# Transposing K and a mixed activation by DMA instead of by TensorE in a fused sparse-attention and MLP-mixer kernel

## The chip, the cores and the metric

The kernel runs on one core of one Trainium2 chip. The metric is device time in microseconds of one execution. A profiled execution also has a span, from its first to its last instruction, which is a little shorter than its time. The engines are TensorE (PE, with its weight loads PEld), VectorE (DVE), ScalarE (ACT), GpSimd (POOL) and SyncE (SP). Each takes its instructions strictly in program order. SP issues all loads of q, k and v and all stores here; POOL issues the weight loads, because these cast from float32 to float16 on the way; 16 DMA engines carry out both.

## What is computed

Four batches, eight heads, 768 positions, head size 64. Attention is causal and sparse by blocks of 64 keys: each query keeps its own block and the three blocks whose mean key has the largest product with it. The result is fed to a token-mixing and a channel-mixing MLP.

```python
k_rep = k.reshape(B, H, n_blocks, block, D).mean(axis=3)
gate_scores = np.einsum('bhsd,bhnd->bhsn', q, k_rep)
gate_scores = np.where(causal, gate_scores, -1000000000.0)
top_idx = np.argsort(gate_scores, axis=-1)[..., -top_k:]
# mask: own block and the top_k blocks, and position i >= position j
scores = scale * np.matmul(q, k.transpose(0, 1, 3, 2))
scores = np.where(mask, scores, -1000000000.0)
attn = softmax(scores);  x = (attn @ v), heads side by side      # (B, 768, 512)
h = np.maximum(x.transpose(0, 2, 1) @ w_tok1, 0.0) @ w_tok2      # 768 -> 256 -> 768
u = x + h.transpose(0, 2, 1)
h2 = np.maximum(u @ w_ch1, 0.0) @ w_ch2                          # 512 -> 1536 -> 512
return u + h2
```

Inputs and output are float32; the matrix products of the kernel run in float16, except the gate and the transposes of q and k, which are float32.

## The kernel before

**Tiles and stages.** Heads are worked in 16 pairs, i = 0 to 15, four to a batch. For each pair:

- SP loads k and q of the pair (`load_qk`, line 244), each as two DMAs of 192 KB, one for each head, with 256 bytes to a row and head, and v as one DMA of 384 KB (`load_v`, line 253).
- TensorE turns k and q around, six 128x128 float32 transposes each (line 269); ScalarE copies the result out of PSUM into `kt` or `qt` (line 278, two buffers of each); GpSimd casts each head's half into the float16 tiles K and Q that the score matmuls read (line 284).
- VectorE sums `kt` over blocks of 64 keys (`ksum`, line 292) and puts the sums into `ks` (`kcopy`, line 300). The gate is five groups of small float32 matmuls (line 310). VectorE adds the causal bias (line 318), takes the eight largest (line 327), compares with the third (line 334) and makes a float16 bias (line 342), which TensorE transposes (`mask`, line 353) and VectorE copies into the free rows of Q (`put_mask`, line 361). The matching rows of K hold indicators of the blocks, so that the score matmul adds the bias itself.
- Scores come in three groups for each head (line 375), each followed by an exponential on ScalarE (line 388), a triangle mask on VectorE (`diag`, line 395; for pair 0 on TensorE, line 379), the product with v (line 406), and the normalization on VectorE (lines 414, 425).

When a batch's four pairs are done, token mixing follows (`tok1` line 437 and `umix` line 449; for batch 0 in column pieces, lines 468 and 482), then u = x + mix on VectorE (`uadd`, line 457; batch 0 line 491). TensorE transposes u in four steps of six 128x128 float16 transposes (`utr`, line 499), VectorE copies them out (`uput`, line 507). Channel mixing reads uT: 24 groups of `ch1` for a batch (line 518), with their relu on ScalarE or VectorE (lines 528, 530), and 18 groups of `ch2` (line 539), an addition on VectorE (line 547) and the store (line 551). The mixing of one batch is meant to lie beside the attention of the next: it fills TensorE where attention waits for its exponentials. For batch 3 there is no attention left to lie beside.

**What sets the order.** The program order is not the order of the code. `plan` (line 64) is a list scheduler that runs while the program is being built. Every piece of work is an `Op` with an engine, a planned occupation, its dependencies, a priority and the buffers that it takes; `plan` goes through planned time, and on each engine it starts the ready piece of the best priority. The order that comes out is the program order of each engine. The chip then does not choose again: an instruction whose input is late holds everything behind it on its engine. DMAs are planned as one queue, in the order of their planned starts, each with a planned size in time; the names SP and SPO both end up on SyncE. [...]

**Start and end.** `dummy` (line 558) fills TensorE at the start with matmuls of no use (up to `WARM` = 120, until planned time `WARM_END`), which the plan takes at 109 ns each; 79 of them are in the program, 34 ahead of the first transpose. GpSimd sets parts of K and Q to zero first (lines 761 to 768). The weights of the token mixer (lines 570, 571) and of the channel mixer (lines 573, 575) are loaded from GpSimd, at points in its order behind casts of pair 3 and later pairs; two lines (662, 663) keep, in the plan only, the loads of pair 4 behind the second weight load.

Of the kernel before, what the change touches and what calls it, by code (L numbers as in the profile page):

```python
# [9 lines left out]
FP = mybir.dt.float32  # L10
F16 = mybir.dt.float16
# [19 lines left out]
TRI = 1  # L31
EARLY = 1
LEAD = 960.0
WARM, WARM_END = 120, 17000.0
IDLE = 1e9
# [123 lines left out]
def kernel(  # L159
# [24 lines left out]
    sp = ctx.enter_context(tc.tile_pool(name="sb", bufs=1))  # L184
    pp = ctx.enter_context(tc.tile_pool(name="ps", bufs=1, space=bass.MemoryType.PSUM))

    pairs = [(b, h) for b in range(B) for h in range(0, H, 2)]
# [19 lines left out]
    QA = [[sp.tile([128, S], F16, tag=f"Q{r}{x}", name=f"Q{r}{x}") for x in range(2)] for r in range(R)]  # L207
    KAX = [sp.tile([128, R, S], F16, tag=f"K{x}", name=f"K{x}") for x in range(2)]
    KA = [[KAX[x][:, r, :] for x in range(2)] for r in range(R)]
    ks2 = [sp.tile([128, 2 * NB], FP, tag=f"ks{r}", name=f"ks{r}") for r in range(R)]  # L210
# [50 lines left out]


    def transposes(t32, i):
        def f():
            p = ps("big", None, f"t{t32}")
            T["tr", t32, i] = p
            t = T[t32, i]
            for j in range(NJ):
                nc.tensor.transpose(out=p[:, 128 * j:128 * j + 128], in_=t[:, j, :], identity=ident32)  # L269
        return f  # L270

    def evac_t(t32, i):
        def f():
            name = "qt" if t32 == "ql" else "kt"
            t = sb(name, [128, S], FP, f"{name}_{i}")
# [287 lines left out]
    for n in range(WARM):  # L563
        wb.users.append(pe(109, [], IDLE, dummy(n), [wb] if n == 0 else []))
    wq = []
# [12 lines left out]
    for i in range(NP):  # L578
# [7 lines left out]

        for t32, src, off in (("kl", k, 0), ("ql", q, 0.1)):
            bf = Buf(t32)
# [70 lines left out]
    for n, (at, f) in enumerate(wq):  # L659
        after = O["cast", "kt", 3, 1] if n < 2 else O["cast", "qt", 3 + (n - 2) // 2, 1]  # L660
        W.append(op("POOL", 700, 0, [after], at, f, size=2900))
    for t32 in ("kl", "ql"):
        O[t32, FIRST].deps.append(W[1])

    for b in range(B):
# [76 lines left out]
    with tc.manual_schedule():  # L742
# [16 lines left out]
        for x in range(2):  # L759
            lo = 64 * (1 - x)  # L760
            nc.gpsimd.memset(KAX[x][lo:lo + 64, :, :].bitcast(FP), 0.0)
        nc.vector.memset(QA[0][0][64:128, :], 0.0)
# [6 lines left out]
        for r in range(R + 1):  # L769
            nc.vector.memset(V16[r][:, :, :, 64:65], 1.0)  # L770
        tri = const("tri", (MASKV * (1.0 - m0_np)).astype(np.float16), F16, nc.scalar)
        m0 = const("m0", np.stack([m0_np, m0_np], axis=1), F16, nc.scalar)
        ind_dram = nc.inline_tensor(np.ascontiguousarray(np.broadcast_to(ind_np[:, None, :], (NB, R, S))), name="indc").ap()
        for x in range(2):
            lo = 64 * (1 - x)
            nc.scalar.dma_start(out=KAX[x][lo:lo + NB, :, :], in_=ind_dram)

# [35 lines left out]
```

## Time and profile before

| | |
|---|---|
| three runs | 281.8, 286.43 and 286.5 us; median 286.43 |
| the profiled execution | 283.26 us, of which its span is 281.4 us |
| granted TensorE clock, mean | 1.00 |
| TensorE busy | 269.9 us, 96% of the span, 2399 matmuls |
| VectorE, ScalarE, GpSimd busy | 168.6, 142.7 and 78.8 us |
| DMA, SP's queue | 78608 packets, 25.17 MB, 40.7% of 16 engines' span |
| DMA, GpSimd's queue | 3232 packets, 3.93 MB, 8.4% |

The profile page gives busy time by engine, the span in 40 slices with the busy share of each in tenths, the DMA queues, the chain of work that ended last, and the costliest groups of instructions. A group's line has the source line, engine, operation, tiles and shapes, the count, then busy time and mean duration of one, then the idle time of that engine just before these instructions and what ended it. Matmuls overlap one another, so that the mean duration of one is longer than the time by which each moves TensorE on; the pieces of the chain of waits give the latter.

### The profile page before, as it was taken

The numbers are of one execution on the slowest core, as the hardware profiler recorded it, in microseconds if no ns is written. First come the engines' busy times: TensorE is split into PE (matmuls) and PEld (weight loads), VectorE is DVE, ScalarE is ACT, GpSimd is POOL, SyncE is SP. The second block draws the span as 40 slices with busy tenths as digits, with TensorE's granted clock in tenths as the row PEclk, the third lists the DMA queues.
The fourth block names the chain that finished last, engine by engine and source line by source line (L and its number), as shares of the span: only waits on it lengthen the run. The fifth ranks groups of instructions, "written<-read, shape, count | busy, mean of one in ns | idle before, by whom it ended". The sixth has DMA issues, their size and how long they took to land.

```text
span 281.4 us, 6095 instructions
## 1 busy us (share of the span) xinstructions
PE 269.9 (96%) x2399; PEld 180.7 (64%) x2399; DVE 168.6 (60%) x573; ACT 142.7 (51%) x188; POOL 78.8 (28%) x102
## 2 busy tenths in 40 slices
PE   8999799889999999999999999999999999999994
PEld 6987488756778777777786545655455545455543
DVE  4478858897679777979999533336323164233222
ACT  2367977288888998888676703440014410044100
POOL 7577702965443375445422000000000000000000
PEclk9999999999999999999999999999999999999999
DMA  8999999999959499570001111000240001120032
GB/s 174 214 214 224 187 222 211 181 225 194 224 112 170 92 213 201 115 168 2 3 0 40 40 75 75 2 0 0 78 148 0 0 2 75 76 77 0 0 125 101
DMA packets 82780, 29.96 MB, mean 106 GB/s; under 512 B 76200, under 2 KB 79272, under 8 KB 82752
## 3 DMA queue, kind: packets, MB, share of 16 engines
q1 hardware_dynamic: 78608, 25.17, 40.7%
q0 software_dynamic: 3232, 3.93, 8.4%
q10 hardware_dynamic: 912, 0.47, 0.8%
q8 instruction: 19, 0.31, 0.5%
q14 instruction: 9, 0.07, 0.1%
HBM read 27.21 MB, written 6.29 MB: 119 GB/s over the span
## 4 chain that ended last, share of the span: by engine, by line
PE 76%; DVE 14%; POOL 2%; DMA 2%; issue 2%; ACT 2%; DVEq 0%; ACTq 0%; POOLq 0%
PE c L539 21%; PE c L518 21%; PE sps L375 7%; PE aps L406 5%; PE warm L558 4%; PE gps L310 3%; DVE e L395 3%; PE tok L437 3%; PE tkl L269 3%; DMA w<-in_moe_w_tok_dram 2%; PE tql L269 2%; PE ups L449 2%; DVE Q L361 2%; DVE kst L292 2%; PE utps L499 2%
## 5 line engine op out<-in xcount | busy, mean ns | idle before, releaser
L388 ACT ACTIVATE e<-sps 128x1024 f16<-128x1024 f32 (+1 forms) x96 | 84.0, 917 | 16.4 <-PE sps L375 11.1
L518 PE MATMUL c<-uT,wc 128*128 128x256 f16 (+1 forms) x384 | 67.9, 326 | 0.2 <-ACT h L528 0.2
L528 ACT ACTIVATE h<-c 128x512 f16<-128x512 f32 x48 | 28.7, 597 | 74.5 <-PE c L518 64.4
L539 PE MATMUL c<-wc,h 128*128 128x512 f16 (+2 forms) x300 | 65.8, 370 | 0.0
L518 PEld LDWEIGHTS <-wc 128*128 128x128 f16 x384 | 37.3, 98 | 24.2 <-issue 0.4
L375 PE MATMUL sps<-Q,K 128*128 128x512 f16 (+3 forms) x256 | 49.9, 305 | 2.2 <-ACT e L388 1.5
L539 PEld LDWEIGHTS <-h 128*128 128x128 f16 x300 | 28.4, 98 | 29.5 <-issue 0.6
L284 POOL CAST K<-kt 64x768 f16<-64x768 f32 x32 | 26.8, 839 | 58.7 <-ACT kt L278 52.4
L530 DVE TENSOR_SCALAR h<-c 128x256 f16<-128x256 f32 x48 | 20.2, 420 | 35.1 <-PE c L518 35.1
L395 DVE TENSOR_TENSOR e<-e,m 128x256 f16<-128x256 f16 x90 | 31.1, 353 | 14.1 <-ACT e L388 13.5
L547 DVE TENSOR_TENSOR ob<-u,c 128x512 f32<-128x512 f16 (+2 forms) x25 | 16.6, 665 | 33.7 <-PE c L539 33.7
L375 PEld LDWEIGHTS <-K 128*128 128x128 f16 x256 | 22.3, 100 | 16.6 <-ACT e L388 2.0
L284 POOL CAST Q<-qt 64x768 f16<-64x768 f32 x32 | 27.0, 843 | 8.8 <-ACT qt L278 7.4
L406 PE MATMUL aps<-V,e 128*128 128x65 f16 x672 | 27.6, 193 | 0.9 <-DVE e L395 0.7
L406 PEld LDWEIGHTS <-e 128*128 128x128 f16 x672 | 25.6, 98 | 3.5 <-DVE e L395 1.5
L278 ACT COPY kt<-tkl 128x768 f32<-128x768 f32 x16 | 12.8, 799 | 17.4 <-PE tkl L269 7.0
L310 PEld LDWEIGHTS gps<-ks,qt 128*128 128x128 f32 x160 | 19.1, 192 | 2.7 <-DVE ks L300 1.3
L310 PE MATMUL gps<-ks,qt 128*128 128x24 f32 x160 | 20.1, 268 | 0.5 <-ACT qt L278 0.3
L425 DVE TENSOR_TENSOR x<-aps,rc 128x384 f16<-128x384 f32 x32 | 17.7, 553 | 0.6
L361 DVE COPY Q<-bps 12x640 f16<-12x640 f16 x32 | 15.5, 484 | 1.3 <-PE bps L353 0.4
L278 ACT COPY qt<-tql 128x768 f32<-128x768 f32 x16 | 12.8, 800 | 5.0 <-PE tql L269 4.3
L292 DVE TENSOR_REDUCE kst<-kt 128x12 f32<-128x768 f32 x15 | 14.1, 943 | 0.8 <-ACT kt L278 0.8
(52 smaller groups left out, 238.3 us busy)
## 6 DMA issues: line engine op xcount, KB each, us to landing
kl<-in_k_dram SPq DMA_DIRECT2D x32, 192.0 KB, 4.5
ql<-in_q_dram SPq DMA_DIRECT2D x32, 192.0 KB, 4.3
v<-in_v_dram SPq DMA_DIRECT2D x16, 384.0 KB, 5.3
out_dram<-ob SPq DMA_DIRECT2D x23, 256.0 KB, 2.0
wc<-in_moe_w_ch_dram POOLq DMA_DIRECT2D x8, 384.0 KB, 6.9
w<-in_moe_w_tok_dram POOLq DMA_DIRECT2D x2, 384.0 KB, 7.0
out_dram<-ob SPq DMA_DIRECT2D x1, 160.0 KB, 1.8
K<-indc ACTq DMA_DIRECT2D x2, 72.0 KB
```

Of the source, the lines that this page charges most:

```text
L278: nc.scalar.copy(out=t, in_=p[:, 0:S])
L284: nc.gpsimd.tensor_copy(out=dst[i % R][x][lo:lo + 64, :], in_=T[name, i][lo:lo + 64, :])
L310: nc.tensor.matmul(out=g[:, j, :], lhsT=T["qt", i][:, 128 * j + 128:128 * j + 256], rhs=ks2[i % R], start=True, stop=True)
L361: nc.vector.tensor_copy(out=QA[i % R][x][lo:lo + NB, 128:S], in_=T["bps", i][lo:lo + NB, :])
L375: nc.tensor.matmul(out=p[:, off + a:off + a + n], lhsT=KA[i % R][x][:, 128 * kk:128 * kk + 128], rhs=QA[i % R][x][:, q0 + a:q0 + a + n], s ...
L388: nc.scalar.activation(out=e[:, 0:width], in_=T["sps", i, x, g][:, 0:width], func=AF.Exp, scale=scale)
L395: nc.vector.tensor_tensor(out=d, in0=d, in1=m0, op=ALU.mult)
L406: nc.tensor.matmul(out=p[:, jq, :], lhsT=T["e", i, x, g][:, o:o + 128], rhs=V16[i % (R + 1)][:, x, kk, :], start=(kk == 0), stop=(kk == jq))
L518: nc.tensor.matmul(out=p, lhsT=wc1_16[:, cc, 128 * fc:128 * fc + 128], rhs=T["uT", b][:, cc, a:e], start=(cc == 0), stop=(cc == NCC - 1))
L528: nc.scalar.activation(out=T["h2", b][:, fc, a:e], in_=T["c1", b, fc, n], func=AF.Relu)
L530: nc.vector.tensor_scalar(out=T["h2", b][:, fc, a:e], in0=T["c1", b, fc, n], scalar1=0.0, scalar2=None, op0=ALU.max)
L539: nc.tensor.matmul(out=T["c2", b, j, lo], lhsT=T["h2", b][:, fc, 128 * j:128 * j + 128], rhs=wc2_16[:, fc, lo:hi], start=(fc == 0), stop=( ...
```

## The change

For pairs 6 to 15 (`VIA` = 6), k no longer goes through TensorE's transposes. It is loaded with eight consecutive rows to a partition (96 partitions, 2 KB to a row and head). VectorE sums the eight rows (`ksum8`), and one small float32 matmul with a constant 0/1 matrix `blk` finishes the sums over blocks (`ksum_pe`). GpSimd casts k into a padded tile K16 of 256 columns to a position: head 0, its indicator columns and zeros, then zeros and indicator columns, then head 1 (`cast_k8`). SP stores that tile to a scratch in DRAM (`store_k`, 384 KB), and one DMA with transpose (`turn_k`) brings it back as both K tiles of the pair, indicator rows included. The next load of k into a `kt` buffer, the cast and the sums thus share the two `kt` buffers with the kt copies of pairs 0 to 5, which still go the old way.

For batches 1 to 3 (`UVIA` = 1), u is stored to a scratch in DRAM (`store_u`, 768 KB) and brought back transposed by one DMA (`turn_u`); their `utr` and `uput` are gone. `ch1` of these batches waits for that DMA.

All new DMAs are issued by SP, among its loads and stores. In the plan the first 20 fillers now occupy 213 ns instead of 109, so that 61 are in the program instead of 79, 18 of them ahead of the first transpose instead of 34. The two lines that kept the loads of pair 4 behind a weight load in the plan are gone. K becomes one tile instead of two, and its zeroing eight instructions instead of two; two K16 tiles are zeroed and given their indicators at the start of GpSimd's program, and GpSimd loses two casts of 64x768 a pair.

```diff
+VIA = 6
+UVIA = 1
-WARM, WARM_END = 120, 17000.0
+WARM, COLD, WARM_END = 120, 20, 17000.0
...
-    KAX = [sp.tile([128, R, S], F16, tag=f"K{x}", name=f"K{x}") for x in range(2)]
-    KA = [[KAX[x][:, r, :] for x in range(2)] for r in range(R)]
+    KAX = sp.tile([128, R, 2, S], F16, tag="KA", name="KA")
+    KA = [[KAX[:, r, x, :] for x in range(2)] for r in range(R)]
+    K16 = [sp.tile([96, 8, 256], F16, tag=f"K16{y}", name=f"K16{y}") for y in range(2)]
...
+    def load_k8(i):
...
+            t = sb("kt", [128, 2, 8, D], FP, f"k8_{i}")[0:96]
+            T["k8", i] = t
+            nc.sync.dma_start(out=t.rearrange("p g t d -> p g (t d)"),
+                              in_=k[b, h:h + 2].rearrange("g (p t) d -> p g (t d)", t=8))
...
+    def ksum8(i):
...
+            t = sp.tile([96, 2, D], FP, tag="kp", bufs=2, name=f"kp_{i}")
+            nc.vector.tensor_reduce(out=t, in_=T["k8", i].rearrange("p g t d -> p g d t"), axis=AX.X, op=ALU.add)
...
+    def ksum_pe(i):
...
+            p = ps("bank", [128, NB], "kps")
+            nc.tensor.matmul(out=p, lhsT=T["kp", i].rearrange("p g d -> p (g d)"), rhs=blk, start=True, stop=True)
...
+    def cast_k8(i):
...
+            nc.gpsimd.tensor_copy(out=K16[y].rearrange("p t (g c) -> p g t c", g=4)[:, 0:4:3, :, :], in_=T["k8", i])
...
+    def store_k(i):
...
+            t = dram.tile([S, 256], F16, tag=f"ks{i % 2}", name=f"kscr_{i}")
+            nc.sync.dma_start(out=t.rearrange("(p t) c -> p (t c)", t=8), in_=K16[i % 2].rearrange("p t c -> p (t c)"))
...
+    def turn_k(i):
+        return lambda: nc.sync.dma_start_transpose(out=KAX[:, i % R, :, :], in_=T["kscr", i])
...
+    def store_u(b):
...
+            t = dram.tile([S, DM], F16, tag=f"us{b % 2}", name=f"uscr_{b}")
+            nc.sync.dma_start(out=t.rearrange("(j p) c -> p j c", p=128), in_=T["u", b])
...
+    def turn_u(b):
+        def f():
+            T["uT", b] = sb("uT", [128, NCC, S], F16, f"uT_{b}")
+            nc.sync.dma_start_transpose(out=T["uT", b], in_=T["uscr", b])
...
-        wb.users.append(pe(109, [], IDLE, dummy(n), [wb] if n == 0 else []))
+        wb.users.append(pe(213 if n < COLD else 109, [], IDLE, dummy(n), [wb] if n == 0 else []))
...
-        for t32, src, off in (("kl", k, 0), ("ql", q, 0.1)):
+        if i >= VIA:
+            kb = Buf("kt")
+            ld = op("SP", 500, 0, [], pre - 12, load_k8(i), [kb], size=1400)
+            O["ksum", i] = dve(1100, [ld], pre + 1, ksum8(i))
+            nb = Buf("bank")
+            O["kpe", i] = pe(115, [O["ksum", i]], pre + 1, ksum_pe(i), [nb])
+            O["kcopy", i] = dve(260, [O["kpe", i], O.get(("gate", old))], pre + 1, kcopy(i))
...
+            O["castk", i] = op("POOL", 1150, 1200, [ld, O["ki", y], O.get(("kst", i - 2))], pre + 3, cast_k8(i))
+            kb.users += [O["ksum", i], O["castk", i]]
+            O["kst", i] = op("SPO", 600, 0, [O["castk", i], O.get(("cast", "kt", i, 0))], pre + 3.1, store_k(i), size=1600)
+            O["kturn", i] = op("SPO", 600, 0, [O["kst", i]] + last_scores(0) + last_scores(1), pre + 3.2, turn_k(i), size=2500)
+            O["cast", "kt", i, 0] = O["cast", "kt", i, 1] = O["kturn", i]
+        for t32, src, off in (("kl", k, 0), ("ql", q, 0.1))[i >= VIA:]:
...
-    for t32 in ("kl", "ql"):
-        O[t32, FIRST].deps.append(W[1])
...
-        for cc in range(NCC):
+        if b >= UVIA:
+            O["ust", b] = op("SPO", 600, 0, uadds[0], early, store_u(b), size=3000)
+            O["uturn", b] = op("SPO", 600, 0, [O["ust", b]], early, turn_u(b), [tb], size=3500)
+            ub.users.append(O["ust", b])
+        for cc in range(NCC if b < UVIA else 0):
...
-                O["ch1", b, fc, n] = pe((864, 436)[n], [O["uput", b, cc] for cc in range(NCC)] + W[2:6],
+                O["ch1", b, fc, n] = pe((864, 436)[n], ([O["uturn", b]] if b >= UVIA else [O["uput", b, cc] for cc in range(NCC)]) + W[2:6],
```

More of the change, by code (lines that the diff above doesn't have):

```diff
@@ L185 @@
     pp = ctx.enter_context(tc.tile_pool(name="ps", bufs=1, space=bass.MemoryType.PSUM))
+    dram = ctx.enter_context(tc.tile_pool(name="dr", bufs=1, space=bass.MemoryType.DRAM))
     pairs = [(b, h) for b in range(B) for h in range(0, H, 2)]
@@ L260, in cast_v, with f, k16_zero, k16_ind @@
         return f
+    def load_k8(i):
+        b, h = pairs[i]
+        def f():
[3 more added lines that the diff above has]
+                              in_=k[b, h:h + 2].rearrange("g (p t) d -> p g (t d)", t=8))
+        return f
+    def ksum8(i):
+        def f():
+            t = sp.tile([96, 2, D], FP, tag="kp", bufs=2, name=f"kp_{i}")
+            T["kp", i] = t
+            nc.vector.tensor_reduce(out=t, in_=T["k8", i].rearrange("p g t d -> p g d t"), axis=AX.X, op=ALU.add)
+        return f
+    def ksum_pe(i):
+        def f():
+            p = ps("bank", [128, NB], "kps")
+            T["kst", i] = p
+            nc.tensor.matmul(out=p, lhsT=T["kp", i].rearrange("p g d -> p (g d)"), rhs=blk, start=True, stop=True)
+        return f
+    def cast_k8(i):
+        def f():
+            y = i % 2
+            nc.gpsimd.tensor_copy(out=K16[y].rearrange("p t (g c) -> p g t c", g=4)[:, 0:4:3, :, :], in_=T["k8", i])
+        return f
+    def store_k(i):
+        def f():
+            t = dram.tile([S, 256], F16, tag=f"ks{i % 2}", name=f"kscr_{i}")
+            T["kscr", i] = t
+            nc.sync.dma_start(out=t.rearrange("(p t) c -> p (t c)", t=8), in_=K16[i % 2].rearrange("p t c -> p (t c)"))
+        return f
+    def turn_k(i):
+        return lambda: nc.sync.dma_start_transpose(out=KAX[:, i % R, :, :], in_=T["kscr", i])
+    def k16_zero(y):
+        return lambda: nc.gpsimd.memset(K16[y].bitcast(FP), 0.0)
+    def k16_ind(y):
+        def f():
+            for c in (64, 128):
+                nc.gpsimd.tensor_copy(out=K16[y][:, :, c:c + NB],
+                                      in_=blk.rearrange("p (o n) -> p o n", o=1).broadcast_to([96, 8, NB]))
+        return f
+    def store_u(b):
+        def f():
+            t = dram.tile([S, DM], F16, tag=f"us{b % 2}", name=f"uscr_{b}")
+            T["uscr", b] = t
+            nc.sync.dma_start(out=t.rearrange("(j p) c -> p j c", p=128), in_=T["u", b])
+        return f
+    def turn_u(b):
+        def f():
+            T["uT", b] = sb("uT", [128, NCC, S], F16, f"uT_{b}")
+            nc.sync.dma_start_transpose(out=T["uT", b], in_=T["uscr", b])
+        return f
     def transposes(t32, i):
@@ L274, in f @@
             name = "qt" if t32 == "ql" else "kt"
-            t = sb(name, [128, S], FP, f"{name}_{i}")
+            t = sb(name, [128, S if name == "qt" else 1024], FP, f"{name}_{i}")[:, 0:S]
             T[name, i] = t
@@ L585, in last_scores @@
             return [O.get(("sc", old, x, g)) for g in range(3)]
-        for t32, src, off in (("kl", k, 0), ("ql", q, 0.1)):
+        if i >= VIA:
[5 more added lines that the diff above has]
+            O["kcopy", i] = dve(260, [O["kpe", i], O.get(("gate", old))], pre + 1, kcopy(i))
+            nb.users.append(O["kcopy", i])
+            y = i % 2
+            if i < VIA + 2:
+                O["kz", y] = op("POOL", 1100, 1150, [], pre - 1, k16_zero(y))
+                O["ki", y] = op("POOL", 400, 450, [O["kz", y]], pre - 1, k16_ind(y))
+            O["castk", i] = op("POOL", 1150, 1200, [ld, O["ki", y], O.get(("kst", i - 2))], pre + 3, cast_k8(i))
[4 more added lines that the diff above has]
+        for t32, src, off in (("kl", k, 0), ("ql", q, 0.1))[i >= VIA:]:
             bf = Buf(t32)
@@ L760 @@
             lo = 64 * (1 - x)
-            nc.gpsimd.memset(KAX[x][lo:lo + 64, :, :].bitcast(FP), 0.0)
+            for r in range(R):
+                nc.gpsimd.memset(KAX[lo:lo + 64, r, x, :].bitcast(FP), 0.0)
         nc.vector.memset(QA[0][0][64:128, :], 0.0)
@@ L771 @@
         tri = const("tri", (MASKV * (1.0 - m0_np)).astype(np.float16), F16, nc.scalar)
+        blk = const("blk", (np.arange(96)[:, None] // 8 == nidx[None, :]).astype(np.float32), FP, nc.scalar)
         m0 = const("m0", np.stack([m0_np, m0_np], axis=1), F16, nc.scalar)
@@ L775 @@
             lo = 64 * (1 - x)
-            nc.scalar.dma_start(out=KAX[x][lo:lo + NB, :, :], in_=ind_dram)
+            nc.scalar.dma_start(out=KAX[lo:lo + NB, :, x, :], in_=ind_dram)
         for o in order:
```

## The prediction

> **What bounds the kernel now.** I read the page first (busy shares, slices, chain), then the chain in order of time, then DMA landings and windows where TensorE has gaps.
>
> ```profile
> PE 269.9 (96%) x2399; PEld 180.7 (64%) x2399; DVE 168.6 (60%) x573; ACT 142.7 (51%) x188; POOL 78.8 (28%) x102
> PE   8999799889999999999999999999999999999994
> DVE  4478858897679777979999533336323164233222
> DMA  8999999999959499570001111000240001120032
> PE 76%; DVE 14%; POOL 2%; DMA 2%; issue 2%; ACT 2%; DVEq 0%; ACTq 0%; POOLq 0%
> ```
>
> TensorE is the bound: 96% busy, and full from 80 us on. Its idle time lies in 20 to 80 us, where the DMA engines are also full. So a matmul less is time less, if nothing new stops TensorE.
>
> ```profile
> 1.07 6.43 PE warm L558 x34
> 7.50 0.66 PE tkl L269 x6
> 28.81 6.29 DMA w<-in_moe_w_tok_dram
> 35.15 0.84 PE tok L468 x12
> ```
>
> These pieces of the chain give what an instruction group moves TensorE on by: 0.66 us for the six transposes of one k. The 34 fillers cost 189 ns each, and later ones 109 (11 in 1.20 us). Weights issued at 28.81 hold TensorE until 35.15.
>
> ```profile
> 231.35 0.34 PE utps L499 x6
> 235.28 11.22 PE c L539 x52
> 246.50 3.57 PE c L518 x21
> ```
>
> The same view near batch 3: 0.34 us for six transposes of u, and 11 us of other work between the last of them and the first reader of uT.
>
> ```profile
> q0 software_dynamic: 818, 1.30, 64.7%
> q1 hardware_dynamic: 4292, 1.08, 50.4%
> v<-in_v_dram SPq DMA_DIRECT2D x1, 384.0 KB, 13.3
> kl<-in_k_dram SPq DMA_DIRECT2D x2, 192.0 KB, 11.9
> ```
>
> The DMA view of 33 to 44 us. While GpSimd's queue (q0) brings in weights, SP's queue (q1) crawls: v of pair 4, issued at 30.9 (timeline of SP), lands 13.3 us later, at 44.2; the next DMA, k of pair 6, issued at 33.2, lands at 45.1. Undisturbed, such loads take 4 to 5 us. Nobody waits for k of pair 6 now; its transposes come later.
>
> ```profile
> 59.00:69.30 10.30, 8.71 (x114) 6.54 (x115) 8.63 (x36) 8.75 (x11) 5.72 (x7) 1.00 1.12 201
> 52.00:62.00 10.00, 7.71 (x89) 5.77 (x87) 9.40 (x42) 6.16 (x8) 8.45 (x11) 1.00 1.12 200
> ```
>
> Two windows (length, then busy PE, PEld, DVE, ACT, POOL). Here attention runs with no or little mixing work beside it, and TensorE is busy for 85% and 77%.
>
> **The change part by part**, on the profiled execution: span 281.4, time 283.26, 1.86 around the span. It lies 3.2 below the median of 286.43.
>
> *Work taken from TensorE.* Ten k transposes x 0.66 = -6.6. Twelve u transposes x 0.34 = -4.1. Ten small float32 matmuls: the nearest row is the gate (ten in 1.08 us, 0.11 each); at most one matmul's full 0.27; I take +1.1, ends 1.1 and 2.7. Eighteen fewer fillers: at 109 ns -2.0, at 189 ns -3.4; I take -2.0, since the first k lands at 5.2 and TensorE cannot start on it sooner than 2.1 before now. Sum -11.6.
>
> *Other engines.* ScalarE loses ten copies of 0.80, GpSimd per pair two casts of 0.84 against one of about 1.1 (1024 elements at the 836 ns for 768 of the v cast). VectorE exchanges the 0.94 sum for one of 1024 elements, 1.15 by the same rate (strided: bound below by 0.94, above by twice), and loses 12 copies of 0.55. None of this is on the path, with one exception, next.
>
> *The wait that the change adds.* In the changed program order `ksum_pe` of pair 6 stands on TensorE ahead of the second half of pair 2's products with v, of all but one score group of pair 3, and of all token mixing of batch 0. On VectorE, `ksum8` of pair 6 stands ahead of pair 2's last triangle mask. Both wait for k of pair 6, which is on SP's queue just behind v of pair 4, as before, behind the same bytes and the same four weight loads. Its 384 KB are contiguous in 2 KB pieces, but they queue. So I expect it at about 45.1, as k of pair 6 now. Then 1.15 of `ksum8` and about 0.15 of handing over: TensorE goes on at 46.4. When does it arrive there? Now it comes to `tok` at 33.6 (35.15 less the 1.5 that it waits). Up to `ksum_pe` it has in addition five score groups (1.9), one transpose group (0.66), two products with v (1.3) and waits for exponentials of about 1.5, less 2.0 of fillers: 37.0. Stall +9.4. The weight wait of 1.5 goes (-1.5), while ScalarE's copies for pair 4 are now late behind the stall: one copy, +0.8. The filler gain is thus swallowed: TensorE reaches a wait that ends at a fixed time.
> Nothing in the trace shows TensorE after so long a silence (its longest wait is 1.5). The nearest row is its start: 25 fillers in the 4.4 us from 1.07 to 5.5, against 2.7 at the later 109 ns. Slow start +1.7, ends 0 and 1.7; I take 1.7.
> The Trainium skill ("TensorE: Matmul & The Clock Gate", Part 1) says that TensorE's clock is halved after an idle window of about 3.4 us and restored after one of work. The clock column shows 1.00 throughout, even over the slow first fillers, so only the durations agree. By the rule the price would be up to 1.7 too.
>
> *Mixing work runs out.* Attention of pairs 6 to 9 stands later in the new order, behind k's detour, and batch 0's mixing earlier: all its `ch1` stand before pair 7's scores, where they reached to pair 12. Its last `ch2` stands inside pair 10; the first `ch1` of batch 1 comes inside pair 12. Between lie 18.4 us of TensorE work (15 score groups, 5 products with v, 2 gates, 2 tok, 6 umix and small things) without filling. At 85% that costs 3.3 more, at 77% 5.5. Besides, pair 14's `mask` stands directly behind its gate: the chain gate to bias now lasts 2.2 (66.5 to 68.7 in VectorE's timeline) and was covered. I take 5.5 + 2.0 = 7.5, ends 3.3 and 9.
>
> *The transposing DMAs.* No row shows one. Lower bound: as 256-byte packets at the mean of SP's queue (40.7% of 281.4 us for 78608 packets: 23.3 ns on one of 16 engines), 2.2 us for a K pair and 4.5 for u. Upper: written in pieces of 32 bytes at the same time each, 18 and 36. I take the lower, as the bytes and rows are nearest to those loads. Cover: a pair takes about 10 us by then, and its other DMAs 6.2 (q 2.0, v 2.0, k and store about 1.0 each), so a K transpose up to about 4 us costs nothing. For u of batch 3, 17 us lie between the last `ups` (229.5) and `ch1` (246.5), less 1.4 of removed transposes. Store about 4, two output stores that SP issues first and that wait for `ch2` until about 236, then 4.5 + 2: landed at 243. Slack about 2.5. Cost 0; beyond that one to one.
> The Trainium skill ("VectorE: DVE Perf Modes", The three transpose paths) gives 1309 ns for a 128x128 DMA transpose against 390 on TensorE, which speaks against the change: twelve blocks one by one would be an estimated 15.7 us, near the upper bound, and the queue would then set the time. "DMA: Bandwidth & Descriptors" (Latency and other measured facts) gives 261 GB/s, an estimated 1.5 us, with no cost. No run shows either yet.
>
> Sum: 281.4 - 11.6 + 9.4 - 1.5 + 0.8 + 1.7 + 7.5 = 287.7; with 1.86 around it 289.6 us, 6.3 above the profiled time.
>
> **Rivals.**
> *A, not slower: k of pair 6 is there in time.* Place: that one load. For it: 2 KB pieces, and DMA has gaps in a few slices. Against: SP's queue was full up to it. Without stall, slow start and late copy, the weight wait back: 289.6 - 9.4 - 1.7 - 0.8 + 1.5 = 279.2. Each us that it lands earlier is a us less; 6.3 earlier, at 38.8, the change is neutral.
> *B, half the stall*: weights of GpSimd come later or share more evenly, landing at 41: 289.6 - 4.1 = 285.5.
> *C, slow transposes.* At 6 us a K pair, 2 us over its cover for nine pairs, 18 more: 307; at 5 us 298. For it: no row; against: the bytes.
> *D, neither wait*: 281.4 - 11.6 + 1.86 = 271.7, TensorE's saving in full. Against: the static order.
>
> **How the numbers follow.** Forecast 0.50 (own range 286 to 293, from the ends of its terms), A 0.12, B 0.17, C 0.15, D 0.06. About 2% is what a measurement of this kernel can tell from no change; against 283.26 that is 277.6 and 288.9. Faster: D and a third of A, 0.10. Slower: four fifths of the forecast and C, 0.55. Within: the rest, 0.35. The range 278 to 303 leaves out D and the slower half of C, 0.14. If runs fall on the level of 286.4 instead, all is 3 higher.
>
> **What would show it.** Right: a TensorE gap of about 9 us near 37 to 46, ended by `ksum_pe` (VectorE: by the DMA of k); TensorE busy about 258; gaps again around pairs 10 to 12; K and u transposes that nobody waits for. Wrong: no gap there, or TensorE waiting for K or uT behind DMA, or a landing of a transpose over 5 us a pair.

## The result, and the profile after

The changed kernel takes 300.61 us in the median of four runs (299.25 to 302.24), against 286.47 (281.8 to 287.17) for the kernel before beside it. The ratio is 1.0624, with a 95% interval of 1.0491 to 1.0757: slower by about 6%. The direction was forecast and the range held the time, but the forecast of 289.6 was 11 us too low. The profiled execution took 299.61 us, its span 297.7; between the profiled executions the loss is 16.4 us, where 6.3 were forecast. Some runs of a kernel show a lower granted clock and take longer: the ratios here leave such runs out, the medians do not, which moves a median below by up to 0.9 us.

From the page of the changed kernel: busy times, the slices of TensorE, of its granted clock and of DMA, and the shares of the chain.

```profile
PE 265.6 (89%) x2269; PEld 173.0 (58%) x2269; DVE 172.9 (58%) x561; ACT 133.2 (45%) x178; POOL 74.9 (25%) x104
...
PE   7898812998799999999986899999999999999995
...
PEclk9999975799979999999999799999999999999999
DMA  9999999899999978899799902900032003820023
...
PE 66%; DVE 19%; DMA 5%; SPq 4%; ACT 3%; issue 2%; DVEq 0%; ACTq 0%
```

The clock column of the kernel before:

```profile
PEclk9999999999999999999999999999999999999999
```

TensorE falls from 96% to 89%, with a hole in slices 6 and 7 and smaller ones near 80 and 165 us, and in or just behind those slices its clock column, 9 throughout before, shows 5 to 7 (tenths of full speed). The chain now has VectorE at 19% in place of 14. DMA is nearly full to about 170 us, where it was full to 77 and had breaks from there on.

The chain in order of time (start, length, what) through the hole:

```profile
32.55 7.68 SPq L257
...
40.32 7.61 DMA k<-in_k_dram
...
47.95 1.90 DVE kp L281
...
49.89 0.60 PE kps L288 x2
...
51.65 1.33 PE tql L336 x6
```

SP needs 7.68 us to issue v of pair 4 behind the weight loads; only then can it issue k of pair 6, which lands at 47.93. The sum takes 1.90, and `ksum_pe` starts at 49.89. In TensorE's timeline that instruction is preceded by 11.20 us of idle time. Afterwards six transposes of q take 1.33 us where six took 0.66 before.

Groups of the changed kernel (count, then busy time and mean ns of one, then idle time before them and what ended it):

```profile
L281 DVE TENSOR_REDUCE kp<-k 96x128 f32<-96x1024 f32 x10 | 19.1, 1905 | 10.1 <-DMA k<-in_k_dram 10.1
...
L288 PE MATMUL kps<-blk,kp 96*128 96x12 f32 x20 | 3.8, 265 | 14.3 <-DVE kp L281 13.9
```

The sum takes 1905 ns, not the 1150 that was taken. Each of the ten sums takes two matmuls on TensorE, not one: twenty, 3.8 us.

Windows of the changed kernel (length, then busy PE, PEld, DVE, ACT, POOL with counts, clock, DMA share, GB/s; the DMA share comes out above 1 in places and is read only as full or not):

```profile
38.00:50.00 12.00, 0.80 (x7) 0.39 (x5) 2.05 (x2) 1.11 (x2) 1.99 (x2) 0.65 1.02 197
50.00:52.00 2.00, 2.00 (x26) 2.00 (x27) 0.84 (x6) 0.71 (x1) 1.17 (x2) 0.50 1.14 264
52.00:54.00 2.00, 1.97 (x9) 1.23 (x8) 1.65 (x4) 0.86 (x2) 0.77 (x2) 0.50 0.38 152
54.00:56.00 2.00, 2.00 (x13) 1.69 (x12) 0.94 (x2) 1.55 (x2) 1.94 (x3) 0.71 0.95 218
```

After the silence TensorE is busy all the time, at half clock for some 5 us. The same happens twice again, after waits of only 2.18 and 2.53 us for the masks of pairs 6 and 14:

```profile
80.00:82.00 2.00, 0.04 (x1) 0.00 (x0) 2.00 (x6) 1.02 (x1) 1.65 (x2) 1.00 1.13 75
82.00:84.00 2.00, 1.78 (x20) 1.34 (x21) 1.96 (x15) 0.38 (x1) 0.00 (x0) 0.62 0.99 178
84.00:86.00 2.00, 2.00 (x19) 1.18 (x17) 1.71 (x7) 1.34 (x2) 0.00 (x0) 0.53 1.30 188
...
164.00:166.00 2.00, 1.81 (x11) 1.12 (x12) 1.33 (x4) 0.35 (x1) 0.01 (x1) 0.60 1.28 290
166.00:168.00 2.00, 1.51 (x7) 0.39 (x5) 1.99 (x3) 2.00 (x3) 0.00 (x0) 0.55 1.13 191
```

Waits of TensorE from 75 to 200 us (total, times, longest):

```profile
PE bps L420 <- DVE bn L409: 4.7, 2, 2.5
PE kps L288 <- DVE kp L281: 2.7, 4, 1.1
```

The forecast had one uncovered mask; there are two. The sums hold TensorE up four more times, for pairs 10, 12, 13 and 14. No wait names the K or uT that come by DMA. Their landings, from the DMA view (last column: median us from issue):

```profile
KA<-kscr SPq DMA_TRANSPOSE x10, 5.8
...
uT<-uscr SPq DMA_TRANSPOSE x3, 7.2
```

### The profile page after: what moved, and what is told of

The parts are those of the page before. It is cut to its first block, busy times and chain, and to the rows that moved or that the text cites. A ratio compares the mean times of both kernels' runs of the same rounds, so it can differ in the third digit from the quotient of the medians.

```text
span 297.7 us, 5828 instructions
## 1 busy us (share of the span) xinstructions
PE 265.6 (89%) x2269; PEld 173.0 (58%) x2269; DVE 172.9 (58%) x561; ACT 133.2 (45%) x178; POOL 74.9 (25%) x104
## 3 DMA queue, kind: packets, MB, share of 16 engines
q1 hardware_dynamic: 93472, 37.76, 59.2%
## 4 chain that ended last, share of the span: by engine, by line
PE 66%; DVE 19%; DMA 5%; SPq 4%; ACT 3%; issue 2%; DVEq 0%; ACTq 0%
PE c L585 20%; PE c L606 19%; PE sps L442 7%; PE aps L473 5%; DVE kp L281 5%; PE gps L377 4%; PE tql L336 3%; SPq L257 3%; DMA k<-in_k_dram 3%; DVE m L394 2%; DVE u L524 2%; PE tok L504 2%; DVE e L462 2%; ACT e L455 2%; DMA ql<-in_q_dram 1%
## 5 line engine op out<-in xcount | busy, mean ns | idle before, releaser
L455 ACT ACTIVATE e<-sps 128x1024 f16<-128x1024 f32 (+1 forms) x96 | 83.1, 922 | 35.2 <-PE sps L442 31.6
L442 PE MATMUL sps<-Q,KA 128*128 128x512 f16 (+3 forms) x256 | 51.9, 318 | 2.0 <-ACT e L455 1.8
L442 PEld LDWEIGHTS <-KA 128*128 128x128 f16 x256 | 24.1, 103 | 19.8 <-issue 3.9
L462 DVE TENSOR_TENSOR e<-e,m 128x256 f16<-128x256 f16 x90 | 28.1, 320 | 10.3 <-ACT e L455 9.9
L473 PE MATMUL aps<-V,e 128*128 128x65 f16 x672 | 28.5, 197 | 1.0 <-DVE e L462 0.7
L473 PEld LDWEIGHTS <-e 128*128 128x128 f16 x672 | 26.8, 100 | 3.9 <-DVE e L462 1.3
L281 DVE TENSOR_REDUCE kp<-k 96x128 f32<-96x1024 f32 x10 | 19.1, 1905 | 10.1 <-DMA k<-in_k_dram 10.1
L377 PEld LDWEIGHTS gps<-ks,qt 128*128 128x128 f32 x160 | 19.9, 195 | 4.0 <-ACT qt L345 2.0
L263 POOL CAST V<-v 128x768 f16<-128x768 f32 x16 | 13.3, 832 | 15.8 <-DMA v<-in_v_dram 15.6
L288 PE MATMUL kps<-blk,kp 96*128 96x12 f32 x20 | 3.8, 265 | 14.3 <-DVE kp L281 13.9
```

What stands on the lines that cost most here:

```text
L281: nc.vector.tensor_reduce(out=t, in_=T["k8", i].rearrange("p g t d -> p g d t"), axis=AX.X, op=ALU.add)
L377: nc.tensor.matmul(out=g[:, j, :], lhsT=T["qt", i][:, 128 * j + 128:128 * j + 256], rhs=ks2[i % R], start=True, stop=True)
L442: nc.tensor.matmul(out=p[:, off + a:off + a + n], lhsT=KA[i % R][x][:, 128 * kk:128 * kk + 128], rhs=QA[i % R][x][:, q0 + a:q0 + a + n], s ...
L455: nc.scalar.activation(out=e[:, 0:width], in_=T["sps", i, x, g][:, 0:width], func=AF.Exp, scale=scale)
L462: nc.vector.tensor_tensor(out=d, in0=d, in1=m0, op=ALU.mult)
L473: nc.tensor.matmul(out=p[:, jq, :], lhsT=T["e", i, x, g][:, o:o + 128], rhs=V16[i % (R + 1)][:, x, kk, :], start=(kk == 0), stop=(kk == jq))
```

## The experiments

The theory after this profile: the static order puts the sums of k of pair 6 in front of work that does not need them, and the DMA behind the weight loads brings that k late; the silence costs the clock besides; and what the sums cost on VectorE and TensorE turns the later attention into short waits. The rival: the scratch stores and transposing DMAs (SP's queue now takes 59.2% of 297.7 us of all 16 engines, 176 us, in place of 114.5) hold up the loads, and the engines merely wait for them. Ratios are to the kernel before, run on the same chip; its median was 284.6 to 286.5 in these series, so that a difference in us between kernels of two series is uncertain by up to 2 us. e1 to e4 are one series, e5 to e8 a second, e9 and e10 a third, e11 and e12 a fourth, e13 and e14 a fifth; the whole change was run apart from them.

| kernel | median us | ratio (95% interval) |
|---|---|---|
| e1_fill: neither detour | 281.55 | 0.9885 (0.9827 to 0.9942) |
| e2_u: u by DMA alone | 276.52 | 0.9709 (0.9640 to 0.9778) |
| e3_k: k by DMA alone | 297.19 | 1.0436 (1.0373 to 1.0498) |
| e4_late: whole change, sum of pair 6 later | 289.51 | 1.0162 (1.0106 to 1.0217) |
| e5_tree: whole change, sum as four additions | 303.74 | 1.0579 (1.0505 to 1.0654) |
| e6_warm: whole change, fillers in the stall | 298.32 | 1.0416 (1.0354 to 1.0477) |
| e7_late_tree: e4 and e5 together | 290.80 | 1.0104 (0.9988 to 1.0220) |
| e8_noturn: e7 without stores and transposes of pairs 8 to 15 | 289.02 | 1.0102 (1.0069 to 1.0136) |
| e9_short: e4 with a cheap sum | 282.81 | 0.9934 (0.9883 to 0.9985) |
| e10_price: e4 planned with the measured prices | 283.99 | 0.9943 (0.9902 to 0.9983) |
| e11_k10: e2 and k by DMA from pair 10 on | 280.68 | 0.9897 (0.9849 to 0.9945) |
| e12_k12: e2 and k by DMA from pair 12 on | 280.48 | 0.9894 (0.9840 to 0.9948) |
| e13_short_warm: e9 with fillers in small gaps | 281.21 | 0.9843 (0.9776 to 0.9910) |
| e14_price_warm: e10 with fillers in small gaps | 281.86 | 0.9866 (0.9797 to 0.9934) |

**e1_fill, e2_u, e3_k: the parts alone.** Both detours off, then one of them on. What is left in e1_fill is fewer fillers, the new tile of K and the plan's missing dependency.

```diff
 e1_fill          e2_u             e3_k
-VIA = 6         -VIA = 6          VIA = 6
+VIA = 16        +VIA = 16        -UVIA = 1
-UVIA = 1         UVIA = 1        +UVIA = 4
+UVIA = 4
```

> Only the fillers and the start-up are changed: k and u go through TensorE as in the kernel before (VIA = 16, UVIA = 4). Forecast's term: 2.0 us less (span 279.4). Rival, from the changed kernel's trace: the first copy on ScalarE still starts at 8.9 us, behind ScalarE's own DMA issues, and the first gate moves from 11.05 to 10.44 only; then 0.6 us or less is gained and the time is the same within 1%.

> Fillers, and u of batches 1 to 3 by DMA; k as in the kernel before (VIA = 16). Theory 1 (the loss lies in k's sums and their place in the order; the transposing DMAs are covered): 12 x 0.34 = 4.1 us less than with the fillers alone, less a wait of up to 2 us for the last uT, so a span of about 277 to 279. Theory 2 (the transposing DMAs and scratch stores hold the kernel up): no gain, TensorE waits several us for uT at each batch, span 282 or more.

> Fillers, and k of pairs 6 to 15 by DMA; u through TensorE as in the kernel before (UVIA = 4). Theory 1: the loss of the whole change is all here, with a stall of 11 us at pair 6 and the halved clock after it; span 296 to 302. Theory 2: the DMA engines carry 6 us per u less each batch, loads and k come sooner, span below 292.

Without either detour 281.55. With u alone 276.52, 5.0 less. With k alone 297.19, 15.6 more. The page of e2_u:

```profile
PE   7779988989999999999999999999999999999995
...
PEclk9999999999999999999999999999999999999999
```

TensorE is full from 80 us on and its clock column is 9 throughout. The transposing DMA of 768 KB is there in time for all three batches:

```profile
uT<-uscr SPq DMA_TRANSPOSE x3, 6.7
```

In e3_k TensorE's timeline has the hole of the whole change (in brackets the idle time before the instruction):

```profile
49.89 0.60 PE L288 MATMUL kps<-blk,kp 96*128 96x12 f32 x2 [9.92 <-DVE kp L281]
```

So the detour of k makes the loss, and that of u is a gain of 5.0 by itself, near the 4.1 of removed transposes. The two do not add up: with k's detour, u by DMA costs another 3.4 us (300.61 against 297.19, from two series, with intervals that touch). In the windows from 140 to 180 us TensorE idles 6.4 us in the whole change and 2.5 in e3_k, and the clock falls only in the former. The u transposes were filling for attention there; without them that attention lies bare. This last is read from the windows, not tried by itself.

**e4_late: the stall.** In the plan alone, the sum of pair 6 is put behind the last scores of pair 3.

```diff
-            O["ksum", i] = dve(1100, [ld], pre + 1, ksum8(i))
+            O["ksum", i] = dve(1100, [ld] + ([O["sc", 3, 1, 2]] if i == VIA else []), pre + 1, ksum8(i))
```

> The whole change, but in the plan alone the sums of pair 6 depend on the last scores of pair 3, so that they stand later in the program order; nothing else of the order is set by hand. Theory 1: the stall of 11.2 us at 38 to 50 us goes, and with it the 2.5 us of halved clock behind it; less what then waits in its place (1 to 3 us): span 285 to 288, against 297.7. Theory 2: the same DMA traffic is there, so a gain of at most 4 us, span 294 or more.

289.51, 11.1 less than the whole change, by an order of work and nothing else. TensorE's wait at `ksum_pe` of pair 6 is 1.26 us now. That shows the stall, with the halved clock and the lost cover behind it, to be worth some 11 us. The scheduler orders everything behind the moved sum anew as well, so the 11 belong to the two orders as a whole; the 9.9 us by which this one wait shrinks are the largest part to be seen. Some 13 remain to e2_u. TensorE's waits in e4_late from 76 to 200 us:

```profile
PE kps L288 <- DVE kp L281: 2.5, 5, 1.1
PE bps L420 <- DVE bn L409: 0.9, 2, 0.5
```

**e5_tree, e7_late_tree: a cheaper sum, which was none.** The strided reduction becomes four contiguous additions, in the whole change and in e4_late.

```diff
-            nc.vector.tensor_reduce(out=t, in_=T["k8", i].rearrange("p g t d -> p g d t"), axis=AX.X, op=ALU.add)
+            a = sp.tile([96, 2, 2, D], FP, tag="kq", bufs=1, name=f"kq_{i}")
+            k8 = T["k8", i]
+            nc.vector.tensor_tensor(out=a, in0=k8[:, :, 0:2, :], in1=k8[:, :, 2:4, :], op=ALU.add)
+            nc.vector.tensor_tensor(out=a, in0=a, in1=k8[:, :, 4:6, :], op=ALU.add)
+            nc.vector.tensor_tensor(out=a, in0=a, in1=k8[:, :, 6:8, :], op=ALU.add)
+            nc.vector.tensor_tensor(out=t, in0=a[:, :, 0, :], in1=a[:, :, 1, :], op=ALU.add)
```

> The whole change, with the sum over the eight rows of a partition made by four contiguous additions (256, 256, 256 and 128 columns) on VectorE in place of one strided reduction of 1024 elements (1.905 us a pair in the profile after). Theory 1, the sums of k on VectorE are on the path: the four additions read contiguously, and by the contiguous sum of 768 elements (0.943 us) 896 columns and three more starts cost about 1.2. So 0.7 us less at the stall of pair 6, and as much of each of the waits at ksum_pe of later pairs (0.27 to 1.10 us, about 3 in all): about 297.5 against 300.6. Theory 2, the full DMA queues hold the kernel back and VectorE only waits for them: 300.6 less at most 0.7 for the stall, 300 or more.

> The whole change with both edits: the sum of pair 6 ordered behind the scores of pair 3, and the four contiguous additions. Theory 1, with the stall gone the sums on VectorE hold the kernel back (VectorE busy 18.5 of 20 us from 60 to 80 us, TensorE waiting 4.3 us in all for the sums): 289.5 less 2 to 5, about 286. Theory 2, DMA holds it back: 289.5 within 0.7.

A miss: 303.74 and 290.80, no gain clear of the intervals in either. The edit did not make the sum cheaper. Its four lines take 18.3 us for ten pairs in e5_tree, 1.83 a pair, against 1.905. VectorE's timeline there, and GpSimd's beside it:

```profile
48.59 0.42 DVE L283 TENSOR_TENSOR kq<-k 96x256 f32<-96x256 f32 x1 [9.67 <-DMA k<-in_k_dram]
49.05 1.14 DVE L284 TENSOR_TENSOR kq<-kq,k 96x256 f32<-96x256 f32 x1
50.22 0.42 DVE L285 TENSOR_TENSOR kq<-kq,k 96x256 f32<-96x256 f32 x1
```

```profile
48.62 1.29 POOL L299 CAST K<-k 96x1024 f16<-96x1024 f32 x1 [1.05 <-DMA k<-in_k_dram]
```

An addition of 256 columns takes 0.42, also the one that begins 0.03 us ahead of GpSimd's cast of the same k; the one that begins while the cast runs takes 1.14, and it ends 0.28 us after the cast does. Five of the thirty additions of 256 columns took 0.92 to 1.14 us, and each of them ended 0.27 or 0.28 us after a cast of GpSimd; the others took 0.40 to 0.43. Four undelayed additions come to 1.54 a pair, still over the 1.2 expected. The Trainium skill ("SBUF — State Buffer", Who interferes with whom) says that a VectorE instruction with two inputs in SBUF contends with a GpSimd instruction that reads SBUF, and that a reduction does not; these rows agree, 1.14 against 0.42 us, and the reduction of pair 6 after the change, which starts 0.03 us ahead of the cast and outlasts it, took 1.88, no more than the mean of ten, 1.905. So these two runs say nothing about what a cheaper sum is worth; e9_short does.

**e6_warm: the clock.** Ninety fillers ahead of `ksum_pe` of pair 6, in the stall.

```diff
-            p = ps("bank", [128, NB], "kps")
+            p = ps("bank", [128, 256], "kps")
+            if i == VIA:
+                for _ in range(90):
+                    nc.tensor.matmul(out=p, lhsT=warm[:, 0:128], rhs=warm, start=True, stop=True)
+            p = p[:, 0:NB]
```

> The whole change, with 90 filler matmuls on TensorE directly ahead of ksum_pe of pair 6, about 9.8 us of work at 109 ns each inside a stall of 11.2. Theory 1, the silence costs TensorE its clock afterwards: the clock stays at 1.00 from 50 to 56 us, and some 2.5 us are gained, 298.1 against 300.6. Theory 2, the low clock in the records of 50 to 55 us costs nothing, since that stretch waits for VectorE or ScalarE anyway: 300.6, or up to 1 more if the fillers outlast the stall.

298.32, near the first expectation, but the intervals (1.0354 to 1.0477, and 1.0491 to 1.0757 for the whole change) do not tell how much of the difference is the clock's, and the profiled execution (299.92) is no shorter than that of the whole change. Two of its windows:

```profile
40.00:60.00 20.00, 18.42 (x223) 15.74 (x221) 10.87 (x35) 7.06 (x9) 7.11 (x9) 1.00 0.99 205
60.00:80.00 20.00, 16.64 (x212) 14.25 (x209) 19.28 (x58) 12.07 (x16) 13.25 (x16) 0.98 1.11 213
```

The clock is 1.00 over the first window, as meant, and TensorE is busy. In the second TensorE idles 3.4 us, against 1.7 in the whole change, but only because everything comes earlier: the wait for the mask of pair 6 is 2.17 us here and 2.18 there, and it ends at 80.47 in place of 82.22, so that 1.7 of it fall into this window. That is a lead of 1.75 us, of which 0.32 was there at `ksum_pe` already (49.57 against 49.89), so the clock kept is worth about 1.4 up to there. Behind this wait the clock is 0.50 from 80 to 86 here, and at the mask of pair 7 the lead has shrunk to 0.63 (86.81 against 87.44); behind the wait for the mask of pair 14 it is low again, 0.50 to 0.67 from 164 to 172, and at 179 us the lead is gone. So in this execution the gain is real where it was aimed at, and later falls of the clock take it back.

**e8_noturn: DMA.** e7_late_tree without the scratch stores and transposing DMAs of pairs 8 to 15.

```diff
-            nc.sync.dma_start(out=t.rearrange("(p t) c -> p (t c)", t=8), in_=K16[i % 2].rearrange("p t c -> p (t c)"))
+            if i < 8:
+                nc.sync.dma_start(out=t.rearrange("(p t) c -> p (t c)", t=8), in_=K16[i % 2].rearrange("p t c -> p (t c)"))
...
+        if i >= 8:
+            return lambda: None
```

> The kernel of e7_late_tree without the scratch stores and the transposing DMAs of pairs 8 to 15 (left out: the scores of these pairs use the transposed k of earlier pairs; everything else is computed as before). Theory 1, these DMAs are hidden and only the sums and the order of the work cost: within 1 us of e7_late_tree. Theory 2, they crowd the DMA engines (share of 0.9 and more from 80 to 160 us, some 4.4 us of all engines a pair) and delay the loads that later work waits for: at least 4 us below e7_late_tree, towards the 276.5 of the kernel with u alone by DMA.

289.02 and a ratio of 1.0102, against 290.80 and 1.0104. The same window of e7_late_tree, then of e8_noturn:

```profile
140.00:160.00 20.00, 18.61 (x176) 12.10 (x173) 15.25 (x57) 9.22 (x12) 6.91 (x8) 1.00 1.00 224
...
140.00:160.00 20.00, 18.16 (x166) 11.28 (x165) 15.30 (x61) 10.48 (x13) 5.78 (x7) 1.00 0.43 100
```

From 140 to 160 us the DMA share is 0.43 where it was 1.00, and the time does not move clear of the intervals (that of e7_late_tree is wide, 0.9988 to 1.0220). The gain of 4 us or more that the rival asked for is not there, so it is out for this order of work and the late pairs; a cost of 1 or 2 us would not show.

**e9_short: what the sum costs.** In e4_late, one addition of two rows in place of the sum of eight.

```diff
-            nc.vector.tensor_reduce(out=t, in_=T["k8", i].rearrange("p g t d -> p g d t"), axis=AX.X, op=ALU.add)
+            nc.vector.tensor_tensor(out=t, in0=T["k8", i][:, :, 0, :], in1=T["k8", i][:, :, 1, :], op=ALU.add)
```

> The kernel of e4_late with the sum over the eight rows of a partition cut to one addition of two of them (left out: the other six rows, so the gate scores of pairs 6 to 15 are of fewer rows). Its price falls from 1.9 us to about 0.29 a pair by the row of the last addition in e5_tree; nothing else moves in the program. Theory 1, VectorE's sum holds TensorE up: the 3.0 us that TensorE waits for the sums between 76 and 200 us, the 1.8 at pairs 6 and 7 and part of the waits for masks and exponentials behind them on VectorE go, 5 us: 284.5 against 289.5. Theory 2, the order of the work leaves too little beside attention, whatever the sum costs: 288 to 289.5.

282.81, 6.7 less than e4_late, more than the 5 expected, although the addition took 0.44 us and not 0.29. The 1.5 us a pair on VectorE that it saves are worth 0.67 a pair of the time. No wait for the sums is left after 75 us. Part of what remains is seen in its windows:

```profile
58.00:60.00 2.00, 1.17 (x17) 0.99 (x17) 1.95 (x7) 0.80 (x1) 1.94 (x4) 1.00 1.11 227
...
62.00:64.00 2.00, 2.00 (x11) 2.00 (x11) 1.20 (x11) 0.00 (x0) 1.00 (x2) 0.50 1.08 184
```

TensorE is busy but at half clock from 62 to 70 us, with no wait ahead of that longer than 0.94 us; in the two microseconds from 58 on it was busy for 1.17.

**e10_price: the plan's prices.** e4_late, planned with the two prices that the trace shows.

```diff
-            O["ksum", i] = dve(1100, [ld] + ([O["sc", 3, 1, 2]] if i == VIA else []), pre + 1, ksum8(i))
+            O["ksum", i] = dve(1900, [ld] + ([O["sc", 3, 1, 2]] if i == VIA else []), pre + 1, ksum8(i))
...
-            O["kpe", i] = pe(115, [O["ksum", i]], pre + 1, ksum_pe(i), [nb])
+            O["kpe", i] = pe(360, [O["ksum", i]], pre + 1, ksum_pe(i), [nb])
```

> The kernel of e4_late with two prices told to the scheduler as the trace has them, 1900 ns for the sum of k on VectorE in place of 1100 and 360 ns for the two small matmuls in place of 115. The work is the same; only its order changes. Theory 1, the order was made for prices that do not hold, so that TensorE reaches the sums, masks and products before VectorE has them: most of the 6 us of such waits between 76 and 200 us go, 284 against 289.5. Theory 2, VectorE or the clock sets the pace and no order helps: 288.5 to 290.

283.99, 5.5 less with the same instructions in another order. Waits of TensorE from 76 to 200 us:

```profile
PE bps L420 <- DVE bn L409: 1.1, 2, 0.6
...
PE kps L288 <- DVE kp L281: 0.2, 1, 0.2
```

The waits for the sums fall from 2.5 to 0.2 us, those for exponentials and products (1.5) go. So the loss that e9_short removes by a cheap sum is probably in large part one of an order made for a cheap sum; the two were not tried together.

**e11_k10, e12_k12: is there a gain left?** e2_u, with k by DMA from pair 10 or 12 on and the prices of e10_price.

```diff
 e11_k10         e12_k12
-VIA = 16       -VIA = 16
+VIA = 10       +VIA = 12
```

> The kernel of e2_u with the keys of pairs 10 to 15 (six pairs) through the scratch, and the two prices of e10_price told to the scheduler; the sums of these pairs come when SP's queue is no longer crowded by the weight loads. Theory 1, apart from the stall, the clock and the wrong prices the detour saves what TensorE sheds, 0.66 us of transposes less 0.36 of small matmuls, 0.3 a pair: 276.5 less 1.8, 274.7. Theory 2, what the detour adds to VectorE (1.9 us against 0.94 a pair) and takes from the order keeps it from paying at all: 276.5 to 279.

> The same with pairs 12 to 15 alone (four pairs). Theory 1: 276.5 less 1.2, 275.3. Theory 2: 276.5 to 278.

280.68 and 280.48: above e2_u by 4 and outside both expectations, so even without the stall the detour costs about 4 us. Six pairs cost no more than four, so this is no price per pair. There is no stall at the first pair, and the clock is at 1.00 from 20 us on. Windows and waits of e12_k12 from 100 to 140 us, where e2_u's TensorE never idles:

```profile
100.00:120.00 20.00, 18.79 (x211) 14.70 (x209) 19.68 (x53) 14.53 (x20) 12.09 (x16) 1.00 1.06 204
120.00:140.00 20.00, 17.45 (x191) 12.21 (x190) 18.38 (x84) 11.66 (x16) 6.10 (x8) 1.00 0.78 153
```

```profile
PE aps L473 <- DVE e L462: 1.4, 2, 0.8
PE bps L420 <- DVE bn L409: 1.2, 2, 0.8
```

VectorE is busy for 19.68 of the first 20 us, and TensorE idles 3.8 us of the forty, waiting mostly for it. The detour takes 0.3 us a pair from TensorE and gives 0.98 to VectorE (1.917 against 0.940 in e12_k12) in the stretch where VectorE has none to spare. That this load is the cause, and not the new order or the DMAs, is read from these waits and was not tried by itself.

**e13_short_warm, e14_price_warm: the clock without a stall.** e9_short and e10_price, with 18 and 19 fillers in gaps of under 1.3 us, by loops like that of e6_warm; e13's:

```diff
+            for _ in range({5: 4, 6: 2, 7: 8}.get(i, 0) if t32 == "ql" else 0):
+                nc.tensor.matmul(out=p[:, 0:256], lhsT=warm[:, 0:128], rhs=warm, start=True, stop=True)
             for j in range(NJ):
...
+            for _ in range({6: 4}.get(i, 0)):
+                nc.tensor.matmul(out=p, lhsT=warm[:, 0:128], rhs=warm, start=True, stop=True)
```

> The kernel of e9_short with 18 filler matmuls in TensorE's small gaps from 53 to 60 us (4 ahead of ksum_pe of pair 6, and 4, 2 and 8 ahead of the transposes of q of pairs 5, 6 and 7), 109 ns each, about as long as the gaps. The sums are cut short as in e9_short. Theory 1, the small gaps there let the clock fall and the low clock of 60.7 to 71 us (0.50) costs about 5 us: the clock stays at 1.00 and 279 is reached against 282.8. Theory 2, the stretch is bound by VectorE and ScalarE and by the order, the clock is only recorded beside it: 282 to 283.

> The kernel of e10_price with 19 fillers (10 and 6 ahead of ksum_pe of pairs 6 and 7, 3 ahead of the transposes of q of pair 5). Theory 1, the low clock of 57 to 68 us (mean about 0.7) costs 3: 281 against 284.0. Theory 2: 284, since VectorE is busy 18 of 20 us there.

281.21 and 281.86, 1.6 and 2.1 less than without the fillers: between the expectations, with intervals that overlap. The profiled executions of these two took 287.06 and 286.26, over the medians, so no time is read from them. Windows of e13_short_warm:

```profile
62.00:64.00 2.00, 1.76 (x22) 1.59 (x21) 1.93 (x15) 0.74 (x1) 1.15 (x2) 1.00 0.87 156
...
68.00:70.00 2.00, 2.00 (x17) 1.07 (x14) 1.90 (x6) 1.70 (x3) 1.09 (x2) 1.00 3.75 194
```

The clock is at 1.00 where it was 0.50: 18 matmuls in small gaps went with that. The 19 of e14_price_warm did not quite: there it still falls to 0.67 and 0.50 from 62 to 66 us. Later in the execution of e13_short_warm something new stands:

```profile
84.55 1.89 PE L447 MATMUL sps<-Q,KA 128*128 128x512 f16 x6 [4.75 <-DMA KA<-kscr]
```

TensorE waits 4.75 us for a transposed K. Of the other profiles only e9_short has such a wait, 0.4 us at a weight load. It stands in one execution that is itself 5.8 us over the median of its kernel, so it does not show that the detour's DMAs hold up the runs of 281 us; it does show that their cover can run out.

**The best version** is e2_u, u by DMA and k as before: 276.52 (276.41 to 276.86), 0.9709 of the kernel before.

## Why the prediction was right and where it was wrong

**The stall** was right in place, cause and order, and too small: a wait of 11.20 us for 9.4. k of pair 6 landed at 47.93 and not at 45.1, since SP issued it only at 40.32, and the sum took 1.9 and not 1.15; TensorE arrived at 38.7 and not at 37.0. In the sum of idle time it comes out even: from 20 to 60 us TensorE idles 8.6 us more than before, and 9.4 - 1.5 + 0.8 had been put down. That is luck in part: the stall was 1.8 longer, while no wait shows the late copy of 0.8, and behind the stall TensorE idles no more up to 60 us, where before the change it idled 1.9 from 40 to 60.

**Mixing work runs out** came out right in total, 7.5 forecast, and from 100 to 200 us TensorE idles 7.5 more (8.3 against 0.8), but by luck in part. The uncovered mask of pair 14 was right, 2.0 forecast and 2.53 measured. Of the other 5.0, though, 2.7 are the waits for the sums, for which the forecast put nothing: it had VectorE's new work off the path "with one exception", the stall. So attention without filling costs about 2.3, not 5.5, and less than the 3.3 of the lower end. From 60 to 100 us there are 2.4 more that no term had, the mask of pair 6 (2.18) above all.

**The transposing DMAs** at no cost were right for the change as made: nobody waits for K or uT, and e8_noturn moves nothing clear of the intervals. Rival C is out, though a K pair lands in 5.8 us, over the 5 that the forecast named as its alarm: landing is not the measure as long as it is early. The 1309 ns a block of the Trainium skill ("VectorE: DVE Perf Modes", The three transpose paths) would make an estimated 15.7 us of a pair's twelve blocks one by one; measured were 5.8 from issue to landing.

**The step that failed is the sum of TensorE's work**, -11.6 with 1.7 of slow start. Span and busy time of the two profiles part the error of 10.0 us (287.7 forecast, 297.7 measured): idle time rose by 20.6 us (281.4 - 269.9 to 297.7 - 265.6) where 16.2 were forecast, and busy time fell by 4.3, to 265.6, where 9.9 were forecast. So 5.6 of the 10.0 lie in TensorE's work:

- *The small matmuls*: 1.1 forecast, 3.8 measured, twice as many and longer; a group of two moves TensorE on by 0.36 us (e4_late). +2.7. The upper bound that the forecast named, 2.7, was exceeded. The gate's row by which they were priced has ten instructions for five matmuls of the program, so by that row ten matmuls are twenty instructions and 2.2 us.
- *The clock*: 1.7 forecast, for one slow start. At most 6.0 measured, from the windows at low clock, each length times what lacks to 1.00: 2.6 at 50 to 56 us, 1.7 at 82 to 86, 1.7 at 164 to 168. +4.3 at most. e6_warm's trace puts the first at about 1.4 of the time, by the lead that TensorE has at pair 6's mask.
- *The fillers* took 3.1 less busy time (12.3 to 9.2 us) where 2.0 were forecast, -1.1, but TensorE idles 2.0 more in the first 20 us. 1.1 of these are a wait for ScalarE's first copy, and the first gate starts at 10.44 in place of 11.05. e1_fill is nevertheless below the kernel before by 1.2% (interval 0.6 to 1.7); where the rest of that comes from was not tried.

These come to 5.9 for 5.6, the clock's part being an upper bound. The other 4.4 are the 2.0 at the start and the 2.4 from 60 to 100 us, two waits that no term had.

**The other rivals.** A and B, k earlier, fell: it came later. D, neither wait, fell for the whole change; of the part with u alone it is true that TensorE's saving arrives in full.

**What stays open.** From the whole change to e2_u are 24.1 us: 11.1 go with the stall (e4_late), 5.5 more with the right prices (e10_price), about 2 with the clock (e14_price_warm), all three steps between series and so good to 2 us each. Of the last 5.3, e11_k10 and e12_k12 make it likely that VectorE's load has a share, since they lose about 4 without a stall and at full clock; but e13_short_warm, whose sum is nearly free, is still 4.7 above. How these divide among VectorE, the order and the K DMAs is not settled.

## What to carry to other kernels

In a statically ordered kernel an instruction that waits for a new DMA costs all that is queued behind it, so ask first where the planner will put the first one of its kind; moving that one by a dependency was worth 11 us here. Before trusting a saving on the busiest engine, price its replacement on the second busiest in the stretch where both are full: 0.3 us a pair saved on TensorE came with 0.98 on VectorE, and the kernel lost 4 us. And give the scheduler measured prices: 1.9 us in place of 1.1 was worth 5.5 us with the same instructions.

## What the runs showed of the hardware

- A reduction of 1024 float32 elements a partition took 1.905 us, 1.86 ns an element, where the eight summed elements lie 64 elements apart; one of 768 elements, where the 64 summed elements lie side by side, took 0.943, 1.23 ns an element. The two differ in their outputs as well, 128 and 12 a partition, so that the distance is the cause is not shown.
- TensorE's clock fell not only after 11.2 us of silence (0.50), but after waits of 2.2 and 2.5 us (0.53 and 0.55), and in e4_late and e9_short to 0.50 with none above 1.3. From e4_late's windows:

```profile
54.00:56.00 2.00, 1.54 (x18) 1.36 (x18) 1.99 (x5) 1.03 (x3) 1.63 (x2) 1.00 0.99 189
56.00:58.00 2.00, 1.34 (x9) 1.04 (x9) 1.83 (x4) 0.74 (x3) 1.66 (x3) 1.00 1.09 216
...
60.00:62.00 2.00, 2.00 (x14) 2.00 (x12) 1.87 (x14) 0.08 (x1) 1.89 (x3) 0.50 1.16 250
```

TensorE was busy 2.88 of the 4 us before 58. The Trainium skill ("TensorE: Matmul & The Clock Gate", Part 1) has the clock halved after an idle window of about 3.4 us and restored after a busy one. The half clock after 11.2 us agrees with that, the falls after short waits do not by that rule alone, and what the page says under "A second HAM failure mode: psum-queue depth-cycling", that frequent small idle times between groups of matmuls let the clock swing, is nearer to them.
- While GpSimd's weight loads ran, SP needed 7.68 us to issue one load of 384 KB, and issued the next at 40.32, behind it. In the kernel before the same load took 2.18 to issue, and the two loads behind it 9.29.
- A transposing DMA from DRAM landed in 5.8 us for 384 KB and 6.7 to 7.2 us for 768 KB (medians), with the DMA engines nearly full for the former.
